# Three engines put in the order of emission, and the w_in conversions cut into five steps: attention, a gated matmul and a soft mixture on one core

## The chip, the cores and the metric

The kernel runs on one core of a Trainium2 chip. The metric is the device time of one execution in microseconds (us); the kernel before was run three times. All times below are of that chip. The engines are TensorE (PE, whose weight loads are listed apart as PEld), VectorE (DVE), ScalarE (ACT), GpSimd (POOL) and SyncE (SP), which here only issues transfers.

## The reference, cut to what matters

```python
# q, k, v: (4, 12, 448, 64) float32; causal attention, then
scores = where(causal_mask, -1e9, q @ k.T / 8)
attn   = exp(scores - max(scores)) / (sum(exp(...)) + 1e-9)
x      = (attn @ v), heads put side by side          # (1792, 768)
h      = x @ w_in                                     # w_in (768, 2048), float64 in memory
g      = maximum(0.01 * h, h)
x      = g @ w_out                                    # w_out (2048, 768), float64 in memory
# soft mixture of 8 experts with 4 slots each
logits = x @ phi                                      # (1792, 32)
d      = softmax over tokens;  slot_input = d.T @ x
slot_out[e] = maximum(slot_input[e] @ w1[e], 0) @ w2[e]
out    = softmax over slots (logits) @ slot_out       # (1792, 768)
```

## The kernel before, in words

**Work.** There are 4 batches of 12 heads. Two heads make a pair, so there are 24 pairs, six to a batch. For a pair `n` the kernel transposes q and k (`qk_stacks`, tile `qkps` in PSUM, `qkt` in SBUF), computes scores once for their maxima (`maxima`: TensorE writes `S`, VectorE reads it into `junk` and the maxima `mxe`), turns the maxima into a row to subtract (`lowering`: `mps`, four ScalarE copies to `mr`), computes transposed scores and their exponentials (`weights`: TensorE writes `T`, ScalarE writes `P`, GpSimd masks the diagonal with an affine select and adds up `tsum`), multiplies by v (`attend`, PSUM tile `O`), inverts the sums (`inverses`: `dn`, a ScalarE copy to `rs`, two VectorE reciprocals) and scales the result into two float16 halves (`columns`: one VectorE product, a ScalarE cast and a GpSimd subtraction into `x`).

**Stages.** Stage 0 does the attention of batch 0. Stages 1, 2 and 3 do the attention of the next batch and, between its parts, `up` of the batch before: 16 column blocks `H` of 18 matmuls each, evacuated by a ScalarE Prelu into `g`. In stages 1 and 2 `g` goes to memory (`g_far`); in stage 3 `up` also adds logits `L` and transposes `g` on VectorE into `g_nat`. After stage 3 come the last `up`, the softmax over tokens, and the experts, whose weights are loaded in 32 transfers of 1.5 MB.

**Slots.** A stage of stages 1 to 3 has 18 slots, three to a pair. I call them A, B and C here. A: `attend(n-1)`, `inverses(n-1)`, `lowering(n)`. B: `maxima` of row block 1, the first part of `weights`, `maxima` of row block 3. C: `columns(n-1)`, the other two parts of `weights`, `maxima` of blocks 0 and 2, `qk_stacks(n+2)`. After each slot follows one column block of `up`, except in the slots 6 and 15 (`GAPS`), which are both slots A.

**Conversions.** w_in and w_out come as float64, and are turned into float32 by integer operations, in 16 units of 128 columns (w_in, names `i0` to `i15`) and 16 of 128 rows (w_out, `o0` to `o15`). `to_f32` does ScalarE Abs (L200) and Sign (L201), for w_in the VectorE maximum (L203), and the VectorE shift (L204) and combination (L205). `prep_in` goes on with `pow2_scale` (a TensorE transposition `w_ps` and five small VectorE operations, L116 to L124), a ScalarE scaling of the sign (L221), a GpSimd product (L222), a ScalarE cast to float16 (L228) and a GpSimd subtraction (L229). `prep_out` multiplies on GpSimd (L238), writes the result to memory, and multiplies it with phi on TensorE (`wt_ps`, `wp_ps`, `wf_ps`) with ScalarE copies between. The units `i6` to `i15` are started in stage 1 (slots 0 to 4 and 6 to 10), `o0` to `o9` in stage 2, `o10` to `o15`, in halves, in stage 3.

**Order.** TensorE runs in the order in which the program emits its instructions: `mm` and `tr` tie each one behind the last. On ScalarE, VectorE and GpSimd a planner sets the order ahead of time, from its own estimate of when each instruction's inputs are ready and from priorities; attention and `up` have a lead of 300 (`AHEAD`). Only the Abs of a conversion (from stage 1 on) and the maximum of v are tied behind what was emitted before them on their engine (`issue_after`). A generator per unit is advanced once per slot by `prep_step`, after the column block; new units are started after that.

**PSUM.** `S` and `T` share two buffers: in a pair they take turns as S(1), T(0), S(3) in slot B and T(1), T(2), S(0,2) in slot C. So S(3) may be written once VectorE has read S(1), and S(0,2) once ScalarE has read T(1). `H` and `O` have one buffer each, and the small tiles (`qkps`, `mps`, `dn`, `w_ps`, `wt_ps` and so on) share two (`TR`).

Of the kernel before, what the change touches and what calls it, by code (L numbers as in the profile page):

```python
# [10 lines left out]
F32 = mybir.dt.float32  # L11
# [23 lines left out]
def tile_attn_moe_softmoe(ctx: ExitStack, tc: tile.TileContext, q, k, v, w_in, w_out, phi, w1, w2, out, dbg=None):  # L35
# [68 lines left out]

    mm = partial(in_order, nc.tensor.matmul)
# [3 lines left out]
    def pow2_scale(absmax, name, shift=23, bias=0, out=None):  # L109
# [6 lines left out]
        nc.vector.tensor_reduce(m1, ps, AX.X, ALU.max)  # L116
        nc.vector.tensor_scalar(m1, m1, as_float((27 + bias) << shift), None, ALU.max)
        e = const.tile([128, 1], I32, tag="p2_e", bufs=2, name=f"{name}_e")
        nc.vector.tensor_scalar(e, m1.bitcast(I32), shift, None, ALU.logical_shift_right)
        si = const.tile([128, 2], I32, tag="p2_s" + name[0], bufs=4, name=f"{name}_s")  # L120
        nc.vector.tensor_scalar(si[:, 0:1], e, -(2**23), (268 + bias) * 2**23, ALU.mult, ALU.add)
        if out is None:
            out = si[:, 1:2].bitcast(F32)
        nc.vector.tensor_scalar(out.bitcast(I32), e, 2**23, -(14 + bias) * 2**23, ALU.mult, ALU.add)  # L124
# [29 lines left out]
    BUFS = ((3, 4, 2), (3, 3, 2), (2, 2, 2))  # L154
# [33 lines left out]
    def to_f32(u, absmax=None):  # L188
# [10 lines left out]
        with tc.issue_after(last_on(mybir.EngineType.Activation)) if stage else ExitStack():  # L199
            nc.scalar.activation(t, hw.bitcast(F32), AF.Abs, scale=2.0**-112)  # L200
        nc.scalar.activation(sg, hw.bitcast(F32), AF.Sign)  # L201
        if absmax is not None:
            nc.vector.tensor_reduce(absmax, t, AX.X, ALU.max)  # L203
        nc.vector.tensor_scalar(ti, ti, 3, None, ALU.logical_shift_left)  # L204
        nc.vector.scalar_tensor_tensor(ti, lw, 29, ti, ALU.logical_shift_right, ALU.bitwise_or)  # L205
# [6 lines left out]
    def prep_in(u):  # L212
# [4 lines left out]
        yield  # L217
        if f >= EARLY[0]:
            yield
        s_w, _ = pow2_scale(am, f"w{f}", 20, out=inv_w[:, f : f + 1])  # L220
        nc.scalar.activation(sg, sg, AF.Copy, scale=s_w)  # L221
        nc.gpsimd.tensor_tensor(t, t, sg, ALU.mult)  # L222
        w = t.rearrange("p (c f) -> p c f", c=NP)
        hi, lo = (w16[f // 4][:, x, :, 128 * (f % 4) : 128 * (f % 4 + 1)] for x in range(2))
        if f < EARLY[0] and f % 4 < HIP:
            nc.gpsimd.tensor_copy(hi, w)
        else:
            nc.scalar.copy(hi, w)  # L228
        nc.gpsimd.tensor_tensor(lo, w, hi, ALU.subtract)  # L229
        ready.add(u[:2])  # L230

    def prep_out(us):

        f, stage = us[0][1], us[0][3]
        wt = None
        for u in us:
            wo, sg = to_f32(u)
            nc.gpsimd.tensor_tensor(wo, wo, sg, ALU.mult)  # L238
# [4 lines left out]
            yield  # L243
            if u[2] is None:
                yield
            if wt is None:
                wt = pools[stage].tile([128, NP, 128], F32, tag="wt", bufs=1, name=f"wt{f}")
            for h in (0, 1) if u[2] is None else (u[2],):
# [18 lines left out]
        ready.add(us[0][:2])  # L267

    ready = set()

    started = [0]
    running = []

# [809 lines left out]
```

## Time and profile before

| | us |
|---|---|
| median of 3 runs | 708.45 |
| the three runs | 708.45, 708.84, 703.36 |
| the profiled execution, its own time | 705.66 |
| its span, first to last instruction | 703.9 |
| TensorE busy (84% of the span) | 592.6 |
| VectorE busy (51%) | 358.0 |
| ScalarE busy (41%) | 289.7 |
| GpSimd busy (34%) | 236.6 |

The mean granted clock of TensorE was 0.951 of full speed. The busy time of an engine is an average over stages that have different limits; a stage is read by who waits for whom in it. In rows of the trace, `xN` is a count, the time in square brackets is the idle time of the engine just ahead of the instruction, and `<-` names what ended it.

### The profile page before, as it was taken

How to read it: one execution, taken by the hardware profiler on the slowest of the kernel's cores; microseconds unless marked ns; L12 is line 12 of the kernel's file. 1: busy time of each engine (PE TensorE's matmuls, PEld its weight loads, DVE VectorE, ACT ScalarE, POOL GpSimd, SP SyncE). 2: the span in 40 equal slices, each digit the busy share in tenths (PEclk: the TensorE clock that was granted, in tenths of full speed). 3: DMA queues.
4: the chain of work that ended last, by engine and by line, in shares of the span. 5: the costliest groups of instructions: out<-in, count | busy, mean ns of one | idle time of the engine just before them, and what ended most of it. 6: DMA issues, size and time to landing. Idle time of an engine off the chain costs nothing.

```text
span 703.9 us, 12298 instructions
## 1 busy us (share of the span) xinstructions
PE 592.6 (84%) x4836; PEld 334.8 (48%) x4836; DVE 358.0 (51%) x884; ACT 289.7 (41%) x571; POOL 236.6 (34%) x247
## 2 busy tenths in 40 slices
PE   3788868877989999899988979999997996998644
PEld 2555544544555555465555545554343443453114
DVE  5868646775764564654645655644555423001004
ACT  1577543656565356465444455442022112011013
POOL 4277743675586342553522434440000000000000
PEclk9999998997989999999999999999999997899798
DMA  9932352542643246663313422206979335999967
GB/s 182 270 99 49 70 173 54 169 129 85 167 145 109 66 150 170 178 189 112 97 49 111 109 81 64 79 24 230 303 279 406 107 146 219 426 423 425 423 259 313
DMA packets 102449, 125.67 MB, mean 179 GB/s; under 512 B 69240, under 2 KB 91256, under 8 KB 98296
## 3 DMA queue, kind: packets, MB, share of 16 engines
q1 hardware_dynamic: 102392, 124.89, 54.2%
q8 instruction: 38, 0.62, 0.4%
q14 instruction: 19, 0.16, 0.1%
HBM read 105.74 MB, written 19.14 MB: 177 GB/s over the span
## 4 chain that ended last, share of the span: by engine, by line
PE 48%; DMA 13%; DVE 11%; ACT 10%; POOL 8%; issue 7%; SPq 1%; ACTq 0%; DVEq 0%; POOLq 0%
PE H L102 22%; DMA w<-in_moe_w_dram 8%; PE O L102 5%; PE g_acc L102 3%; DVE g_nat L608 2%; DVE rs L450 2%; PE S L102 2%; ACT P L408 2%; PE qkps L102 2%; POOL cv_i_None L222 2%; PE ph L941 2%; DMA raw_i_None<-in_moe_w_in_dram 2%; PE dn L102 2%; PE L L102 2%; PE T L102 2%
## 5 line engine op out<-in xcount | busy, mean ns | idle before, releaser
L102 PE MATMUL H<-x,w 128*128 128x448 f16 x1152 | 234.8, 359 | 0.7 <-ACT g L668 0.7
L102 PEld LDWEIGHTS <-w 128*128 128x128 f16 x1152 | 112.5, 100 | 113.4 <-issue 22.5
L372 DVE CUSTOM_DVE_ANT_0 junk<-S,mask 112x224 bf16<-112x224 f32 (+3 forms) x192 | 85.1, 443 | 47.8 <-PE S L102 44.7
L668 ACT ACTIVATE g<-H,iv 128x448 f32<-128x448 f32 x58 | 36.7, 633 | 112.1 <-PE H L102 101.3
L450 DVE RECIPROCAL rs<-rs 128x224 f32<-128x224 f32 x36 | 53.4, 1524 | 38.2 <-ACT rs L448 38.2
L102 PE MATMUL S<-qkt 64*112 64x224 f32 (+3 forms) x192 | 33.8, 393 | 35.0 <-ACT P L408 21.8
L102 PE MATMUL O<-P,v 112*64 112x448 f32 (+3 forms) x384 | 57.4, 444 | 6.1 <-POOL P L412 4.4
L102 PE MATMUL T<-qkt 64*112 64x336 f32 (+3 forms) x576 | 58.4, 315 | 3.9 <-ACT P L408 3.2
L412 POOL TENSOR_SCALAR_AFFINE_SELECT P<-P 112x448 f32<-112x448 f32 x48 | 33.8, 708 | 82.1 <-ACT P L408 69.3
L408 ACT ACTIVATE P<-T 112x672 f32<-112x672 f32 (+1 forms) x72 | 55.8, 791 | 12.1 <-PE T L102 11.8
L485 POOL TENSOR_TENSOR x<-rs,x 128x448 f16<-128x448 f32 x24 | 25.3, 1053 | 84.9 <-ACT x L484 79.6
L102 PEld LDWEIGHTS T<-qkt 64*112 64x112 f32 x576 | 43.1, 180 | 10.4 <-ACT P L408 3.6
L421 POOL TENSOR_TENSOR tsum<-tsum,P 112x448 f32<-112x448 f32 (+1 forms) x48 | 46.4, 967 | 3.1
L102 PEld LDWEIGHTS O<-P,v 112*64 112x64 f32 x384 | 27.5, 148 | 35.2 <-issue 17.6
L1029 PE MATMUL po<-w,hz 128*32 128x384 f32 x256 | 27.3, 548 | 17.7 <-DMA w<-in_moe_w_dram 17.7
L417 POOL TENSOR_TENSOR tsum<-P 112x672 f32<-112x672 f32 x24 | 39.4, 1643 | 1.3
L102 PEld LDWEIGHTS S<-qkt 64*112 64x112 f32 x192 | 16.0, 184 | 50.1 <-ACT P L408 25.6
L933 POOL MEMSET hz<- 128x256 f32 x2 | 0.6, 312 | 109.6 <-PE g_acc L102 109.6
L608 DVE STREAM_TRANSPOSE g_nat<-g 128x448 f32<-128x448 f32 x26 | 16.5, 640 | 37.7 <-ACT g L668 37.7
L350 DVE TENSOR_TENSOR qkt<-qkps,qkt 128x448 fp32r<-128x448 f32 x48 | 28.9, 620 | 10.5 <-ACT qkt L349 10.5
L222 POOL TENSOR_TENSOR cv_i_None<-cv_i_None,cs_i_None 128x768 f32<-128x768 f32 x16 | 28.0, 1747 | 16.8 <-ACT cs_i_None L221 16.8
L384 ACT ACTIVATE mr<-mps,own 128x112 fp32r<-128x112 f32 x96 | 26.2, 361 | 16.0 <-PE mps L102 16.0
(174 smaller groups left out, 865.8 us busy)
## 6 DMA issues: line engine op xcount, KB each, us to landing
w<-in_moe_w_dram SPq DMA_DIRECT2D x32, 1536.0 KB, 20.8
raw_i_None<-in_moe_w_in_dram SPq DMA_DIRECT2D x16, 768.0 KB, 4.6
raw_o_None<-in_moe_w_out_dram SPq DMA_DIRECT2D x10, 768.0 KB, 6.0
g_far<-g SPq DMA_DIRECT2D x32, 224.0 KB, 6.4
gb<-g_far SPq DMA_DIRECT2D x8, 896.0 KB, 6.7
wo<-wsc SPq DMA_DIRECT2D x4, 1536.0 KB, 10.0
qk<-in_q_dram SPq DMA_DIRECT2D x48, 112.0 KB, 2.5
qk<-in_k_dram SPq DMA_DIRECT2D x48, 112.0 KB, 2.9
```

The source lines that it names most:

```text
L102: op(*args, **kwargs)
L222: nc.gpsimd.tensor_tensor(t, t, sg, ALU.mult)
L350: nc.vector.tensor_tensor(st[:, j, 1], p, st[:, j, 0].bitcast(F32), ALU.subtract)
L372: nc.vector.tensor_tensor_reduce(out=junk[:, :w], in0=ps[:, a, at : at + w], in1=mask[:, S - w :], scale=-1.0, scalar=3e38, op0=ALU.add, o ...
L408: nc.scalar.activation(x[:, :, o : o + at], ps[:, :, :at], AF.Exp, scale=SCALE)
L412: nc.gpsimd.affine_select(out=d, in_=d, compare_op=ALU.is_ge, fill=0.0, base=0, pattern=[[0, 4], [1, CP]], channel_multiplier=-1,)
L417: nc.gpsimd.tensor_tensor(tsum[:CP], p[0][:CP, :, 0, CP:], p[0][:CP, :, 1, : S - CP], ALU.add)
L421: nc.gpsimd.tensor_tensor(y, y, p[1][:CP, :, j, : S - CP * (j + 2)], ALU.add)
L450: nc.vector.reciprocal(rs[:, c : c + S // 2], rs[:, c : c + S // 2])
L608: nc.vector.transpose(g_nat[:, :, 32 * f : 32 * (f + n)].rearrange("p c (f x) -> p f c x", x=32), gts[b, f].rearrange("p (c x) -> p c x", ...
L668: nc.scalar.activation(g, ps, AF.Prelu, scale=iv[b][:, f : f + 1], alpha=SLOPE)
L1029: nc.tensor.matmul(po[h][32 * g : 32 * g + 32], hp[:, (t0 + t) % 8], wt[:, t, DH * h - c0 : DH * (h + 1) - c0], start=t0 + t < 4, stop=t0 ...
```

## The change

ScalarE, VectorE and GpSimd instructions go through a wrapper that, from the beginning of stage 1 until the end of stage 3, ties each behind the last one emitted on its engine. In these stages all three engines, like TensorE, run in the order of emission. In stage 0 and after stage 3 the wrapper ties nothing.

`prep_step` gets a phase. In a slot the order of emission is now: the attention part, the steps marked BEFORE, the start of new units, the column block of `up`, the steps marked AFTER. A w_in unit of stage 1 started in slot s does `to_f32` in s, `pow2_scale` in s+1 AFTER, the scaling and the product (L221, L222) in s+3 BEFORE, the cast and the subtraction (L228, L229) in s+4 BEFORE; before, all that follows `to_f32` was done in s+2. A w_in unit of stage 0 does `pow2_scale` in s+1 and the rest in s+2; before, all in s+1. A whole w_out unit does its transpositions one slot earlier, and a w_out unit in halves converts its second half in the next slot BEFORE. The buffers of a conversion in stages 1 and 2 go from 3 to 5 (`cv_t`) and from 2 to 4 (`cv_s`). `columns(n-1)` moves from the beginning of slot C to its end, behind `qk_stacks` and the loads. The slots in which units start are the same as before.

```diff
+    fixed = [False]
+
+    class Ordered:
+        def __init__(self, engine, kind):
+            self.engine, self.kind = engine, kind
+
+        def __getattr__(self, name):
+            op = getattr(self.engine, name)
+
+            def run(*args, **kwargs):
+                with tc.issue_after(last_on(self.kind)) if fixed[0] else ExitStack():
+                    op(*args, **kwargs)
+
+            return run
+
+    scalar = Ordered(nc.scalar, mybir.EngineType.Activation)
+    vector = Ordered(nc.vector, mybir.EngineType.DVE)
+    gpsimd = Ordered(nc.gpsimd, mybir.EngineType.Pool)
...
-    BUFS = ((3, 4, 2), (3, 3, 2), (2, 2, 2))
+    BUFS = ((3, 4, 2), (3, 5, 4), (2, 2, 2))
...
-        with tc.issue_after(last_on(mybir.EngineType.Activation)) if stage else ExitStack():
-            nc.scalar.activation(t, hw.bitcast(F32), AF.Abs, scale=2.0**-112)
-        nc.scalar.activation(sg, hw.bitcast(F32), AF.Sign)
+        scalar.activation(t, hw.bitcast(F32), AF.Abs, scale=2.0**-112)
+        scalar.activation(sg, hw.bitcast(F32), AF.Sign)
...
         t, sg = to_f32(u, am)
-        yield
-        if f >= EARLY[0]:
-            yield
+        yield AFTER
+        yield AFTER
         s_w, _ = pow2_scale(am, f"w{f}", 20, out=inv_w[:, f : f + 1])
-        nc.scalar.activation(sg, sg, AF.Copy, scale=s_w)
-        nc.gpsimd.tensor_tensor(t, t, sg, ALU.mult)
+        yield BEFORE
+        if u[3]:
+            yield BEFORE
+        scalar.activation(sg, sg, AF.Copy, scale=s_w)
+        gpsimd.tensor_tensor(t, t, sg, ALU.mult)
+        if u[3]:
+            yield BEFORE
...
+            wos.append((wo, c0))
+            if u is not us[-1]:
+                yield BEFORE
+        if len(us) == 1:
+            yield AFTER
+        yield AFTER
+        wt = pools[stage].tile([128, NP, 128], F32, tag="wt", bufs=1, name=f"wt{f}")
+        for h in (0, 1):
...
+            if h == 0 and len(us) > 1:
+                yield AFTER
+        yield AFTER
...
-    def prep_step():
-
-        for g in list(running):
-            if next(g, 1) == 1:
-                running.remove(g)
+    def prep_step(phase):
+
+        for x in list(running):
+            if x[1] == phase:
+                x[1] = next(x[0], None)
+                if x[1] is None:
+                    running.remove(x)
...
             yield
-            columns(n - 1)
             if here:
                 weights(n, 1)
                 weights(n, 2)
...
             if n + NP < NPAIR:
                 load_v(n + NP)
+            columns(n - 1)
             if n + NP - 1 < NPAIR:
                 reduce_v(n + NP - 1)
...
             with tc.high_priority(offset=AHEAD):
                 next(slots_of_attention, None)
-                if columns_of_g is not None and x not in GAPS:
+            prep_step(BEFORE)
+            while started[0] < min(count, had + -(-(count - had) * (x + 1) // last)):
+                prep_start()
+            if columns_of_g is not None and x not in GAPS:
+                with tc.high_priority(offset=AHEAD):
                     next(columns_of_g)
-            prep_step()
-            while started[0] < min(count, had + -(-(count - had) * (x + 1) // (slots - (4 if columns_of_g is None or count > NF else 6)))):
-                prep_start()
+            prep_step(AFTER)
...
         load_raw()
+        fixed[0] = True
         for b in range(1, 4):
...
+        fixed[0] = False
```

## Rows read from the trace of the kernel before

**Rows 1.** Busy time by stretch: the transition to stage 1, then stages 1, 2 and 3.

```profile
core 0: us, PE busy (x) PEld busy (x) DVE busy (x) ACT busy (x) POOL busy (x), PEclk, DMA share, GB/s
95.00:109.40 14.40, 9.55 (x89) 7.17 (x89) 6.32 (x21) 6.87 (x13) 5.25 (x7) 0.78 0.63 189
109.40:244.00 134.60, 115.17 (x748) 66.18 (x748) 87.81 (x222) 74.63 (x132) 75.86 (x59) 0.91 0.42 118
244.00:371.10 127.10, 117.77 (x931) 71.08 (x930) 68.16 (x157) 67.41 (x141) 51.97 (x47) 1.00 0.48 135
371.10:481.00 109.90, 101.91 (x782) 58.85 (x782) 61.84 (x134) 52.72 (x117) 39.14 (x43) 1.00 0.28 80
```

**Rows 2.** TensorE's waits in stage 1 and (last) stage 3: total us, times, longest.

```profile
PE S L102 <- ACT P L408: 13.0, 7, 3.0
PE S L102 <- DVE mxe L372: 3.3, 3, 1.5
...
PE S L102 <- ACT P L408: 4.0, 3, 1.5
```

**Rows 3.** Timeline of ScalarE in a slot C of stage 1, and TensorE's wait there.

```profile
145.62 0.88 ACT L200 ACTIVATE cv_i_None<-raw_i_None 128x768 f32<-128x768 f32 x1
...
147.18 0.93 ACT L221 ACTIVATE cs_i_None<-cs_i_None,w_s 128x768 bf16<-128x768 bf16 x1
...
148.19 1.33 ACT L408 ACTIVATE P<-T 112x672 f32<-112x672 f32 x2
...
148.96 0.50 PE L102 MATMUL S<-qkt 64*112 64x112 f32 x4 [3.00 <-ACT P L408]
```

**Rows 4.** Timeline of ScalarE and TensorE at the transition from stage 0.

```profile
102.17 0.89 ACT L201 ACTIVATE cs_i_None<-raw_i_None 128x768 bf16<-128x768 f32 x1 [3.01 <-DMA raw_i_None<-in_moe_w_in_dram]
...
105.14 0.71 ACT L408 ACTIVATE P<-T 112x672 f32<-112x672 f32 x1
...
105.90 0.35 PE L102 MATMUL S<-qkt 64*112 64x224 f32 x2 [2.55 <-ACT P L408]
...
109.44 3.97 PE L102 MATMUL O<-P,v 112*64 112x448 f32 x16 [1.69 <-DVE qkt L350]
```

**Rows 5.** Timeline of TensorE: slot starts and a column block of one pair.

```profile
207.11 2.11 PE L102 MATMUL O<-P,v 112*64 112x448 f32 x16
...
210.06 3.57 PE L102 MATMUL H<-x,w 128*128 128x448 f16 x18
...
213.78 0.36 PE L102 MATMUL S<-qkt 64*112 64x224 f32 x2
...
226.06 2.11 PE L102 MATMUL O<-P,v 112*64 112x448 f32 x16
```

**Rows 6.** What VectorE does for a unit and a pair: timeline and groups, stage 1.

```profile
210.02 0.53 ACT L448 COPY rs<-dn 128x448 f32<-128x448 f32 x1
...
134.44 2.96 DVE L450 RECIPROCAL rs<-rs 128x224 f32<-128x224 f32 x2 [2.51 <-ACT rs L448]
...
131.02 0.29 DVE L116 TENSOR_REDUCE w_m<-w_ps 128x1 f32<-128x128 f32 x1 [0.56 <-PE w_ps L102]
...
131.79 0.14 DVE L124 TENSOR_SCALAR inv_w<-w_e 128x1 int32<-128x1 int32 x1
...
L203 DVE TENSOR_REDUCE w_am<-cv_i_None 128x1 f32<-128x768 f32 x10 | 9.3, 940 | 10.9 <-ACT cv_i_None L200 10.9
...
L204 DVE TENSOR_SCALAR cv_i_None<-cv_i_None 128x768 int32<-128x768 int32 x10 | 8.6, 864 | 0.5
...
L372 DVE CUSTOM_DVE_ANT_0 junk<-S,mask 112x224 bf16<-112x224 f32 x12 | 4.6, 380 | 4.8 <-PE S L102 4.7
```

**Rows 7.** Timeline of GpSimd and VectorE: the same product twice, and a neighbour.

```profile
143.20 1.64 POOL L222 TENSOR_TENSOR cv_i_None<-cv_i_None,cs_i_None 128x768 f32<-128x768 f32 x1 [2.53 <-ACT cs_i_None L221]
...
148.18 2.47 POOL L222 TENSOR_TENSOR cv_i_None<-cv_i_None,cs_i_None 128x768 f32<-128x768 f32 x1 [0.75 <-ACT cs_i_None L221]
148.19 0.96 DVE L205 SCALAR_TENSOR_TENSOR cv_i_None<-raw_i_None,cv_i_None 128x768 int32<-128x768 int32 x1
```

More of the change, by code (lines that the diff above doesn't have):

```diff
@@ L242, in prep_out @@
             )
[L243 to L248, printed above, removed]
-                ps = ps_tr(f"wt_ps{f}_{h}", (128, 3, 128))
-                for j in range(3):
-                    c = 128 * (3 * h + j) - c0
-                    tr(ps[:, j], wo[:, c : c + 128], ident)
-                nc.scalar.copy(wt[:, 3 * h : 3 * h + 3], ps)
-        yield
+            wos.append((wo, c0))
[6 more added lines that the diff above has]
+        for h in (0, 1):
+            wo, c0 = wos[h % len(wos)]
+            ps = ps_tr(f"wt_ps{f}_{h}", (128, 3, 128))
+            for j in range(3):
+                c = 128 * (3 * h + j) - c0
+                tr(ps[:, j], wo[:, c : c + 128], ident)
+            scalar.copy(wt[:, 3 * h : 3 * h + 3], ps)
+            if h == 0 and len(us) > 1:
+                yield AFTER
+        yield AFTER
         psw = ps_tr(f"wp_ps{f}", (96, 128))
@@ L261, in prep_out @@
         w4 = pools[stage].tile([96, 128], F32, tag="w4", bufs=1, name=f"w4_{f}")
-        nc.scalar.copy(w4, psw)
-        yield
+        scalar.copy(w4, psw)
+        yield AFTER
         psf = ps_tr(f"wf_ps{f}", (128, NS))
         mm(psf, w4, istack[:96, :NS], start=True, stop=True)
-        nc.scalar.copy(wprime[:, f], psf)
+        scalar.copy(wprime[:, f], psf)
         ready.add(us[0][:2])
     ready = set()
+    BEFORE, AFTER = "before", "after"
     started = [0]
     running = []
-    def prep_step():
-        for g in list(running):
-            if next(g, 1) == 1:
-                running.remove(g)
+    def prep_step(phase):
[4 more added lines that the diff above has]
+                    running.remove(x)
     def prep_start():
@@ L284, in prep_start @@
         g = prep_in(us[0]) if u[0] == "i" else prep_out(us)
-        next(g)
-        running.append(g)
+        running.append([g, next(g)])
     def need(u):
@@ L330, in reduce_v @@
             v_am[b] = am = const.tile([128, NP + 1], F32, tag="v_am", bufs=2, name=f"v_am{b}")
-            nc.vector.memset(am, 0.0)
-        with tc.issue_after(last_on(mybir.EngineType.DVE)) if b else ExitStack():
-            nc.vector.tensor_reduce(v_am[b][:CP, hp : hp + 1], v_t[n], AX.XY, ALU.max, apply_absolute_value=True)
+            vector.memset(am, 0.0)
+        with tc.issue_after(last_on(mybir.EngineType.DVE)) if b and not fixed[0] else ExitStack():
+            vector.tensor_reduce(v_am[b][:CP, hp : hp + 1], v_t[n], AX.XY, ALU.max, apply_absolute_value=True)
     def v_scale(b):
         am = v_am[b]
-        nc.vector.tensor_reduce(am[:, NP:], am[:, :NP], AX.X, ALU.max)
+        vector.tensor_reduce(am[:, NP:], am[:, :NP], AX.X, ALU.max)
         s_v[b], inv_v[b] = pow2_scale(am[:, NP:], f"v{b}")
@@ L383, in lowering @@
         for i in range(NI):
-            nc.scalar.activation(mr[:, i], ps, AF.Copy, scale=own[:, i : i + 1])
+            scalar.activation(mr[:, i], ps, AF.Copy, scale=own[:, i : i + 1])
     def weights(n, g):
@@ L474, in columns @@
             rs = att.tile([128, S], F32, tag="rs", bufs=1, name=f"rs{n}")
-            nc.scalar.copy(rs, rb)
+            scalar.copy(rs, rb)
         else:
@@ L667, in up @@
             queue.append(f)
[L668 removed]
+            scalar.activation(g, ps, AF.Prelu, scale=iv[b][:, f : f + 1], alpha=SLOPE)
             if far:
@@ L781, in stage @@
         had = started[0]
+        last = slots - (6 if columns_of_g is not None and count <= NF else 4)
         for x in range(slots):
```

127 lines of the change are left out of this document (64 added, 63 removed).

## The prediction, made blind

> **What bounds the kernel now.** I read the busy time by stretch first, then TensorE's waits in each stage, then the timelines of the engines around the longest of them. In stages 1 to 3 TensorE has the most work: 115.2 of 134.6 us, 117.8 of 127.1 and 101.9 of 109.9, while no other of the four is busy for more than 87.8, 68.2 and 61.8 us there [rows 1]. So what the stages can still give is TensorE's idle time, 19.4, 9.3 and 8.0 us, and in stage 1 its clock, 0.91 of full in the mean; it was 1.00 in the other two [rows 1]. After stage 3, from 481 us on, the change ties nothing, so I let that tail move as a whole with the end of stage 3.
>
> The cause of the idle time is visible. TensorE runs in the order written, so a late ScalarE or VectorE result stops all that follows. In stage 1 the wait of S(0,2) for the exponential P is the largest, 13.0 us in 7 waits, and the wait of S(3) for the maxima `mxe` comes next with 3.3 us [rows 2]. A slot C of stage 1 shows the first: ScalarE runs the Abs of a unit and the scaling of another ahead of the two exponentials, which begin at 148.19, and TensorE stands for 3.00 us [rows 3]. The planner had put conversions there. The same happens at the transition: a Sign of a stage 1 unit, which nothing ties, stood in ScalarE's queue in front of an exponential and waited for its transfer [rows 4].
>
> **The transition: about 4.2 us gained.** The Sign waited 3.01 us; the exponential behind it began at 105.14, TensorE waited 2.55 us for it and 1.69 us more ahead of O [rows 4]. With the new order the Sign can't start before the last instruction that stage 0 emitted, so both waits go: 4.2 us. If the exponential finds the next wait at once, only the first goes, 2.5 us. O took 3.97 us there against 2.11 at full clock [rows 4, 5]; if that comes back too the gain is 6.1 us. The granted clock was 0.78 over the whole stretch [rows 1], so I don't count it.
>
> **Stage 1: what goes.** The exponentials now stand ahead of every conversion step of their slot, and the long ScalarE queue in front of them is gone. I take 0.4 us per pair as what is left of that wait, since the exponential follows its scores directly.
>
> **Stage 1: what takes its place.** In the order of emission the VectorE part of a unit started in slot A (L203, L204, L205) and the `pow2_scale` of the unit before stand in front of the maxima of row block 1 in slot B, and S(3) can't be written until these have read S(1). I count from the start of O. A pair with little in its way shows that slot A takes TensorE 6.7 us (207.11 to 213.78) and the pair 18.95 (to 226.06) [rows 5]; less two waits for P of 0.4 us 18.1. The sum copy `rs` starts 2.9 us after O [rows 5, 6]. A copy takes 0.5 and the two reciprocals 2.96, so VectorE has them done at 6.4. L203, L204 and L205 take 0.94, 0.86 and 0.96 [rows 6, 7]: done at 9.2. The five small operations of `pow2_scale` take 0.9 (131.02 to 131.93 [rows 6]): 10.1. Two maxima at 0.38, with their read-outs some 0.45 each [rows 6]: 11.0. TensorE gets to S(3) at 6.7 + 1.2 = 7.9, as S(1) and T(0) take it 1.2. So it waits about 3 us, and H behind it waits as well.
>
> By this I went through the six pairs, with the units that are in each. Pair one (start in slot 0, no `pow2_scale` yet) waits 2.0; pair two 3.0; pair three 5.4, since slot 6 has no column to cover for VectorE, and ScalarE has a cast and a scaling ahead of the Abs; pair four 3.7; pair five, without starts, 0.2; pair six, where slot 15 has no column, 2.7, for the reciprocals alone. Together 17.0. TensorE's own work is six times 18.1 less the two columns that are left out, 3.57 each by the row [rows 5] and 3.4 from start to start: 101.8. To this come 2.4 for the exponentials and 0.9 where `mps` wants the buffer of a `w_ps` that VectorE has not yet read. That makes 122.1 at full clock.
>
> The clock comes on top. [...] Four of the waits above are longer than those of the transition, so 7 to 8 us; I take 7. Stage 1: 129.1 instead of 134.6, **a gain of 5.5 us**. Ends: the waits for the maxima are half as long and the clock stays, 101.8 + 8.5 + 2.4 = 112.7, a gain of 21.9; or every long wait is 1.5 us longer and the clock costs 9, 136, a loss of 1.4.
>
> ScalarE and GpSimd have room: cast, scaling, Abs and Sign cost ScalarE about 0.8 each in sequence (145.62 to 147.18 for two [rows 3]), 3.1 us in a slot of some 6, and a product and a subtraction cost GpSimd 3.3. The five buffers cover the longer life of a unit: started in slot 0 it is ready in slot 4 and wanted in slot 7. That they cost nothing holds as long as the slots keep these lengths; each slot of lateness would use up one of the three in reserve.
>
> **The columns moved to the end of slot C.** Their VectorE product now stands behind the maxima and the two subtractions of `qk_stacks`; the next `attend` needs the buffer O that it reads. Some 2 us of VectorE work follow the transpositions, and the column of 3.4 us covers them. But the cast of `columns` on ScalarE waits for that product, and Abs, Sign and the Prelu of H stand behind it: I find the Prelu late by 1.3 us in slots C with a start.
>
> **Stages 2 and 3: nothing.** In stage 2 w_out units have no L203 and no `pow2_scale`, so S(3) waits 0.2 to 1.2 us in most pairs, and in slots 6 and 15, which have the reciprocals in front as before, 1.0 and 2.5. The late Prelu makes the second `wt_ps` wait for its small buffer, 1.2 to 1.45 us in three slots C. The walk gives 127.5 us against 127.1, so I take 0, with 3 us to either side: below nothing too, as the idle time of 9.3 us [rows 1] could shrink. Stage 3: the waits for P, 4.0 us [rows 2], go, and transpositions of `g` on VectorE, now in fixed places before the maxima, take about as much: 0, again 3 to either side. Stage 0 has its steps moved by a slot and its order made by the planner: 0, 3 to either side.
>
> **SyncE.** The planner still orders the transfers, and every step moved takes its own along. A transfer of `g` waits for a Prelu and holds q and k behind it; those have a whole pair, some 19 us, to arrive. I take 0.
>
> **Sum.** 705.66 - 4.2 - 5.5 = 696.0, made against the profiled execution, which lies 2.8 us below the median of the three runs and between the lowest and the other two. I forecast 696.
>
> **Rivals.**
> *A, the waits go and nothing takes their place (0.20).* If VectorE keeps ahead, stage 1 costs 112.7: 705.66 - 21.9 - 4.2 = 679.6. For it: VectorE is busy for 87.8 of 134.6 us [rows 1], so there is room in the sum. Against it: the room isn't in slot A, where reciprocals, unit and maxima stand in one row.
> *B, an even trade (0.17).* S(3) waits as long as S(0,2) did, the clock falls as often, and only part of the transition is left: 703 to 706.
> *C, slower (0.11).* The maxima of slot B stand behind a unit in stages 2 and 3 too. If a unit ends 1.5 us later there than in my walk, eleven pairs lose 16.5 us: 712.5. From 0.9 us in each pair on (9.7 / 11) the change loses. For it: no start in a slot A can step behind the maxima any more, as the planner let it. Against it: w_out units need only L204 and L205.
> *D, the two engines block each other (0.07).* The same GpSimd product took 1.64 us alone and 2.47 when VectorE began L205 within 0.01 us of it [rows 7]. The new order puts products and subtractions into each slot of a unit's life. If each of the four units started in a slot A finds a whole product of 1.64 us in front of its L205, TensorE loses 6.6 us: 702.6. [...]
>
> **How the numbers follow.** My forecast has 0.45, between 691 and 701. About 1%, 7 us, is what a measurement of this kernel can tell from no change, as its three runs alone differ by 5.5 us. Faster by more: 0.43 of the forecast and all of A, 0.63. Slower by more: 0.09, the larger part of C. Within 1%: 0.28. The range goes from 682, which is nearly A, to 708, which takes in B and D and leaves out most of C.
>
> **What would show it.** In the trace after: at the transition no Sign in front of the exponential, and no wait of 2.5 us there. In stage 1 TensorE's waits for P at 3 us or less in all; its waits for `mxe` at 10 to 20 us, in slots B whose slot A started a unit, longest after slot 6. Stage 1 some 129 us long, its clock still below full; stages 2 and 3 within 3 us of before. The forecast fails if waits for `mxe` stay near 3 us (A), if they appear in stages 2 and 3 at 1.5 us or more per pair (C), or if stage 0 or the tail changes its length by more than 3 us.

## The result and the profile after

The changed kernel takes 689.1 us in the median of four runs (686.7 to 690.9), against 708.6 us of the kernel before: 0.974 of its time, with a 95% interval of 0.968 to 0.979. The forecast was 696.0, with a range of 682 to 708. The profiled execution of the changed kernel took 690.89 us, with a span of 689.2; it is the slowest of its four, and that of before, 705.66, lies below its median. So the two traces differ by 14.7 us, and the medians by 19.5. The account below is that of the traces.

Busy time by stretch, after the change: the transition, then stages 1, 2 and 3 (the columns are those of [rows 1]).

```profile
95.00:105.80 10.80, 8.71 (x91) 6.69 (x91) 5.83 (x20) 5.33 (x11) 5.83 (x7) 0.84 0.77 235
105.80:226.60 120.80, 108.59 (x748) 63.02 (x748) 86.67 (x221) 76.95 (x137) 66.68 (x57) 0.96 0.47 133
226.60:354.80 128.20, 117.32 (x931) 71.06 (x930) 69.50 (x159) 70.00 (x143) 49.70 (x48) 1.00 0.45 134
354.80:466.60 111.80, 105.27 (x782) 59.72 (x782) 61.34 (x134) 52.95 (x118) 39.68 (x44) 0.97 0.27 79
```

Against [rows 1] nearly the whole gain lies in stage 1, which takes 120.8 us instead of 134.6. TensorE's instructions are the same 748, but they take 108.6 us instead of 115.2, as the granted clock is 0.96 instead of 0.91, and its idle time falls from 19.4 to 12.2 us. So of 13.8 us gained some 7 are waiting and some 7 are clock. Stage 1 begins 3.6 us earlier. Stages 2 and 3 are slightly longer, by 1.1 and 1.9 us.

TensorE's waits in stage 1, after the change (total us, times, longest):

```profile
PE S L102 <- ACT P L116: 7.5, 5, 3.5
PE v_ps L102 <- DVE v_am L116: 2.1, 1, 2.1
PE O L102 <- POOL P L116: 1.2, 1, 1.2
PE T L102 <- ACT mr L116: 1.1, 2, 0.5
PE mps L102 <- ACT rs L116: 0.7, 1, 0.7
PE mps L102 <- DVE w_m L116: 0.3, 1, 0.3
```

In the kernel after, L116 is the line of the wrapper, so one goes by the tiles. The wait for P has fallen from 13.0 to 7.5 us [rows 2]. On the timelines, 10.3 of the 13.0 us were waits of S(0,2), in five slots C, and 2.7 were waits of S(3), in two slots B. After the change S(0,2) waits in no slot C, and all five waits for P are those of S(3). The wait for `mxe`, which the forecast put at 17 us, is not there at all. A wait that the forecast didn't know has come: `v_ps` for `v_am`, 2.1 us. The transition and the first slots of stage 1, on the timeline of all engines:

```profile
101.11 0.73 ACT L116 ACTIVATE P<-T 112x672 f32<-112x672 f32 x1 [1.62 <-PE T L102]
...
105.79 2.11 PE L102 MATMUL O<-P,v 112*64 112x448 f32 x16 [1.18 <-POOL P L116]
...
113.45 0.92 ACT L116 ACTIVATE P<-T 112x896 f32<-112x896 f32 x1 [0.40 <-PE T L102]
...
114.42 0.45 PE L102 MATMUL S<-qkt 64*112 64x448 f32 x2 [1.01 <-ACT P L116]
...
114.60 0.38 DVE L116 CUSTOM_DVE_ANT_0 junk<-S,mask 112x224 bf16<-112x224 f32 x1
...
116.78 0.15 DVE L116 TENSOR_REDUCE v_am<-v_am 128x1 f32<-128x6 f32 x1
...
116.99 0.80 PE L102 MATMUL v_ps<-ident,v_am 128*128 128x128 f32 x2 [2.12 <-DVE v_am L116]
```

The exponential of the transition now waits for its scores on TensorE and not behind a Sign, and O begins at 105.79 instead of 109.44, in 2.11 us instead of 3.97 [rows 4]. The lines at 113.45 to 114.60 are one slot B. S(3) is written at 114.42, as the exponential of T(0) ends, and VectorE begins to read S(1) only at 114.60. So S(3) stands in the buffer of T(0), and not in that of S(1). In pairs two, three, four and six it is the same: S(3) is written before VectorE has read S(1). In pair five it is not:

```profile
198.17 0.92 ACT L116 ACTIVATE P<-T 112x896 f32<-112x896 f32 x1 [0.41 <-PE T L102]
...
198.26 0.45 PE L102 MATMUL S<-qkt 64*112 64x448 f32 x2
```

There S(3) is written while ScalarE still reads T(0), so it has the buffer of S(1), which VectorE had read early in this pair without new units.

The longest wait for P that is left is that of the third pair, on ScalarE and TensorE:

```profile
153.63 0.86 ACT L116 CAST w<-cv_i_None 128x768 f16<-128x768 f32 x1
...
154.36 0.97 ACT L116 ACTIVATE cs_i_None<-cs_i_None,w_s 128x768 bf16<-128x768 bf16 x1
...
155.19 0.91 ACT L116 ACTIVATE cv_i_None<-raw_i_None 128x768 f32<-128x768 f32 x1
155.97 0.91 ACT L116 ACTIVATE cs_i_None<-raw_i_None 128x768 bf16<-128x768 f32 x1
...
156.75 0.94 ACT L116 ACTIVATE P<-T 112x896 f32<-112x896 f32 x1
...
157.75 0.71 PE L102 MATMUL S<-qkt 64*112 64x448 f32 x2 [3.46 <-ACT P L116]
```

Four conversion steps stand ahead of the exponential here, 3.1 us in all, after slot 6, which has no column of `up` to cover them.

### The profile page after: what moved, and what is told of

The parts are those of the page before. It is cut to its first block, busy times and chain, and to the rows that moved or that the text cites. A ratio compares the mean times of both kernels' runs of the same rounds, so it can differ in the third digit from the quotient of the medians.

```text
span 689.2 us, 12302 instructions
## 1 busy us (share of the span) xinstructions
PE 590.5 (86%) x4836; PEld 333.7 (48%) x4836; DVE 357.8 (52%) x884; ACT 292.3 (42%) x571; POOL 225.5 (33%) x247
## 4 chain that ended last, share of the span: by engine, by line
PE 57%; DVE 12%; DMA 11%; ACT 7%; POOL 7%; issue 4%; SPq 1%; ACTq 0%; DVEq 0%; POOLq 0%
PE H L102 27%; DMA w<-in_moe_w_dram 8%; PE O L102 5%; PE T L102 3%; PE S L102 3%; PE g_acc L102 3%; DVE rs L116 3%; DVE junk L116 3%; ACT P L116 3%; POOL tsum L116 2%; DVE g_nat L116 2%; PE dn L102 2%; DMA raw_i_None<-in_moe_w_in_dram 2%; PE ph L976 2%; PE L L102 2%
## 5 line engine op out<-in xcount | busy, mean ns | idle before, releaser
L116 DVE CUSTOM_DVE_ANT_0 junk<-S,mask 112x224 bf16<-112x224 f32 (+3 forms) x192 | 85.6, 446 | 78.6 <-PE S L102 73.6
L116 ACT ACTIVATE g<-H,iv 128x448 f32<-128x448 f32 x58 | 36.7, 633 | 107.8 <-PE H L102 83.7
L116 DVE RECIPROCAL rs<-rs 128x224 f32<-128x224 f32 x36 | 53.3, 1523 | 46.5 <-ACT rs L116 46.5
L116 ACT ACTIVATE P<-T 112x672 f32<-112x672 f32 (+1 forms) x72 | 57.1, 793 | 25.8 <-PE T L102 24.8
L116 POOL TENSOR_SCALAR_AFFINE_SELECT P<-P 112x448 f32<-112x448 f32 x48 | 28.4, 592 | 118.4 <-ACT P L116 66.5
L102 PE MATMUL O<-P,v 112*64 112x448 f32 (+3 forms) x384 | 53.1, 417 | 5.6 <-POOL P L116 5.6
L116 POOL TENSOR_TENSOR tsum<-tsum,P 112x448 f32<-112x448 f32 (+1 forms) x48 | 43.2, 899 | 3.3
L1064 PE MATMUL po<-w,hz 128*32 128x384 f32 x256 | 29.2, 580 | 16.4 <-DMA w<-in_moe_w_dram 16.4
L102 PEld LDWEIGHTS O<-P,v 112*64 112x64 f32 x384 | 25.9, 140 | 32.2 <-issue 14.8
L116 POOL TENSOR_TENSOR tsum<-P 112x672 f32<-112x672 f32 x24 | 38.8, 1615 | 1.9
L102 PE MATMUL T<-mr,onesr 64*112 64x448 f32 (+1 forms) x192 | 30.9, 318 | 3.8 <-ACT mr L116 3.8
L116 DVE TENSOR_TENSOR qkt<-qkps,qkt 128x448 fp32r<-128x448 f32 x48 | 27.8, 618 | 10.5 <-ACT qkt L116 10.5
L116 ACT ACTIVATE mr<-mps,own 128x112 fp32r<-128x112 f32 x96 | 26.2, 361 | 14.3 <-PE mps L102 14.3
L116 POOL TENSOR_TENSOR cv_o_None<-cv_o_None,cs_o_None 128x768 f32<-128x768 f32 x10 | 16.5, 1648 | 48.2 <-DVE cv_o_None L116 28.8
L102 PEld LDWEIGHTS S<-qkt 64*112 64x112 f32 x192 | 16.0, 184 | 32.9 <-ACT P L116 13.7
L116 POOL TENSOR_TENSOR w<-cv_i_None,w 128x768 f16<-128x768 f32 x16 | 26.7, 1668 | 10.1 <-ACT w L116 10.0
```

The lines of the kernel that those rows point to most:

```text
L102: op(*args, **kwargs)
L116: op(*args, **kwargs)
L1064: nc.tensor.matmul(po[h][32 * g : 32 * g + 32], hp[:, (t0 + t) % 8], wt[:, t, DH * h - c0 : DH * (h + 1) - c0], start=t0 + t < 4, stop=t0 ...
```

## The experiments

The readings to be told apart were these. The first, of the forecast: what counts is that the exponentials no longer stand behind conversion steps. The first rival: the five steps and the buffers do it, whatever the order. The second: only the transition counts, where one Sign was in the way. A further question is why the waits for `mxe` didn't come. No kernel below leaves out any of the computation.

All eleven experiments beside the two kernels; the lengths are from the traces. The beginning of a stage is that of its first O, in us from the span's start, and stage 3 is counted to the last O. The ratio is to the kernel before, which ran again beside each group of kernels (medians of 707.6 to 708.6 us).

| kernel | median us | ratio (95%) | stage 1 begins | stage 1 | stage 2 | stage 3 |
|---|---|---|---|---|---|---|
| before | 708.6 | | 109.4 | 134.6 | 127.0 | 102.8 |
| after | 689.1 | 0.974 (0.968 to 0.979) | 105.8 | 120.9 | 128.1 | 104.8 |
| order_alone | 792.1 | 1.119 (1.114 to 1.125) | 105.5 | 186.3 | 149.9 | 118.1 |
| steps_alone | 732.1 | 1.037 (1.031 to 1.043) | 110.6 | 131.8 | 137.6 | 118.6 |
| sign_tied | 700.6 | 0.991 (0.988 to 0.994) | 104.3 | 130.6 | 129.8 | 101.8 |
| steps_sign | 707.8 | 1.001 (0.998 to 1.004) | 104.4 | 138.4 | 128.8 | 106.0 |
| stage1_only | 719.0 | 1.015 (1.011 to 1.020) | 103.9 | 121.1 | 144.2 | 117.5 |
| scalar_only | 682.8 | 0.966 (0.960 to 0.972) | 105.6 | 120.8 | 126.2 | 101.4 |
| columns_first | 699.0 | 0.989 (0.982 to 0.995) | 103.7 | 132.0 | 127.1 | 105.1 |
| rotate | 712.6 | 1.005 (1.002 to 1.009) | 113.7 | 132.5 | 132.2 | 103.1 |
| v_early | 678.9 | 0.959 (0.955 to 0.963) | 104.0 | 117.2 | 126.5 | 99.9 |
| scalar_v | 685.2 | 0.967 (0.960 to 0.973) | 105.5 | 118.3 | 126.2 | 101.5 |
| slot5 | 682.4 | 0.963 (0.958 to 0.968) | 104.1 | 120.6 | 126.5 | 99.9 |

**order_alone: the new order with the old steps.** The kernel after, with the steps, the buffers and the place of `columns` of before; the three engines stay in the order of emission.

```diff
-    BUFS = ((3, 4, 2), (3, 5, 4), (2, 2, 2))
+    BUFS = ((3, 4, 2), (3, 3, 2), (2, 2, 2))
...
-        yield AFTER
-        yield AFTER
+        yield
+        if f >= EARLY[0]:
+            yield
         s_w, _ = pow2_scale(am, f"w{f}", 20, out=inv_w[:, f : f + 1])
-        yield BEFORE
-        if u[3]:
-            yield BEFORE
         scalar.activation(sg, sg, AF.Copy, scale=s_w)
         gpsimd.tensor_tensor(t, t, sg, ALU.mult)
-        if u[3]:
-            yield BEFORE
```

> The kernel before with the order of emission alone: its steps, its buffers and the place of the columns as before. Theory 1 (the order alone brings the gain, since it takes the conversions out from in front of the exponentials): 689 to 697. Theory 2 (the order needs the five steps): a unit's scaling, product, cast and subtraction all stand in one slot, and in the order of emission ScalarE's cast waits for GpSimd's product (1.64 us) and the scaling for VectorE, with the next slot's exponentials behind them; 2 to 4 us for each of the ten w_in units: 715 to 735, with the waits of S for P in stage 1 at 20 us or more.

It takes 792.1 us, some 84 more than before and far beyond any of the figures expected. ScalarE in a slot of stage 1, and TensorE's wait there:

```profile
150.08 0.94 ACT L116 ACTIVATE cs_i_None<-cs_i_None,w_s 128x768 bf16<-128x768 bf16 x1 [3.15 <-DVE w_s L116]
...
152.76 0.83 ACT L116 CAST w<-cv_i_None 128x768 f16<-128x768 f32 x1 [1.75 <-POOL cv_i_None L116]
...
155.06 0.90 ACT L116 ACTIVATE P<-T 112x896 f32<-112x896 f32 x1
...
156.02 0.71 PE L102 MATMUL S<-qkt 64*112 64x448 f32 x2 [9.29 <-ACT P L116]
```

Emitted right behind what they need, the scaling waits at the head of ScalarE's queue for VectorE's `w_s`, and the cast for GpSimd's product. The exponential stands behind both, and TensorE waits 9.29 us. In the whole stage its waits for P are 55.6 us in 11 cases, against 7.5 in 5 after. In an order that nothing can step around, each step must find its input ready; that is what the five steps are for. Steps, buffers and the place of `columns` went back together here. columns_first, below, moves only `columns` back and costs 10 us, so most of the loss is that of steps and buffers, which were not taken apart.

**steps_alone: the new steps with the planner's order.** The kernel after without the wrapper's ties; the Abs keeps the tie that it had before.

```diff
-        scalar.activation(t, hw.bitcast(F32), AF.Abs, scale=2.0**-112)
+        with tc.issue_after(last_on(mybir.EngineType.Activation)) if stage else ExitStack():
+            scalar.activation(t, hw.bitcast(F32), AF.Abs, scale=2.0**-112)
...
-        fixed[0] = True
```

> The changed kernel without the order: five steps, more buffers, the columns at the end of slot C, and the planner's order on the three engines, with only Abs and the maximum of v tied as before. Theory 1 (the order brings the gain): 703 to 710. Theory 2 (each half needs the other): 698 to 710, too. Theory 3 (the steps and buffers alone bring it, since no step waits for another engine any more): 687 to 694.

It takes 732.1 us, slower than before, which none of the readings gave; the rival by which the steps alone do it has fallen. Stage 1 is only 2.8 us shorter than before, and stages 2 and 3 are longer by 10.6 and 15.7. ScalarE in stage 2 shows a likely cause, which steps_sign tests:

```profile
263.37 0.89 ACT L116 ACTIVATE cs_o_None<-raw_o_None 128x768 bf16<-128x768 f32 x1 [4.30 <-DMA raw_o_None<-in_moe_w_out_dram]
264.16 0.72 ACT L116 ACTIVATE P<-T 112x672 f32<-112x672 f32 x1
```

This is the Sign of [rows 4] again: untied, it was put in front of an exponential and waited 4.30 us for its transfer.

**sign_tied: the kernel before with one more tie.** The Sign is tied like the Abs, and nothing else is changed.

```diff
-        nc.scalar.activation(sg, hw.bitcast(F32), AF.Sign)
+        with tc.issue_after(last_on(mybir.EngineType.Activation)) if stage else ExitStack():
+            nc.scalar.activation(sg, hw.bitcast(F32), AF.Sign)
```

> The kernel before with the Sign of each conversion of stages 1 to 3 tied behind the last ScalarE instruction emitted, as its Abs is. If the 4 us of the transition come from the Sign alone, O of pair 7 begins 3 to 4.5 us earlier than 109.4 and the time is 702 to 706; if another conversion takes its place in front of the exponential, 707 to 710. Stages 1 to 3 stay within 3 us each.

It takes 700.6 us, less than either figure expected, and the transition is as short as with the whole change:

```profile
99.61 0.73 ACT L409 ACTIVATE P<-T 112x672 f32<-112x672 f32 x1 [1.16 <-PE T L102]
...
104.29 2.11 PE L102 MATMUL O<-P,v 112*64 112x448 f32 x16 [1.18 <-POOL P L413]
```

O begins 5.1 us earlier than before, and stage 1 is 4.0 us shorter. Its waits for P are not: 14.4 us against 13.0. What shrinks is TensorE's busy time, 111.4 us instead of 115.2, at a clock of 0.93 instead of 0.91. Two lines of the source give some 7 of the 19.5 us. The rival "only the transition" accounts for about that part and not for the rest, since stage 1 stays at 130.6.

**steps_sign: the steps, the planner's order, and the Sign tied.** The kernel steps_alone with the tie of sign_tied.

> The changed kernel without the order (as steps_alone), but with the Sign tied as in sign_tied. If steps_alone is slow because the planner puts Signs that wait for their transfers in front of everything on ScalarE: stages 2 and 3 go back to some 128 and 104 us and the time is 700 to 708. If the planner's order on all three engines is at odds with the new steps in other ways too: 715 to 728.

It takes 707.8 us, at the upper end of the lower figure expected. Stages 2 and 3 are back at 128.8 and 106.0, so what steps_alone lost there was the Sign. Stage 1 takes 138.4: with the same steps and buffers the planner's order costs 17.5 us there against the order of emission (120.9). This pair of kernels is the cleanest measure of the order. But it isn't one of exponentials behind conversion steps, as TensorE's waits in stage 1 show (total, times, longest):

```profile
PE S L102 <- ACT P L116: 7.0, 5, 1.7
PE w_ps L102 <- DVE qkt L116: 5.6, 3, 4.7
```

For P TensorE waits no longer than after (7.5). About half of the 17.5 us are other waits, for VectorE and GpSimd, and about half are TensorE's busy time, 117.2 us against 108.6, at a clock of 0.90 against 0.96. The longest wait, on VectorE and TensorE:

```profile
147.81 5.16 DVE L116 SCALAR_TENSOR_TENSOR cv_i_None<-raw_i_None,cv_i_None 128x768 int32<-128x768 int32 x1
...
153.57 0.80 PE L102 MATMUL w_ps<-ident,w_am 128*128 128x128 f32 x2 [4.75 <-DVE qkt L116]
```

A combination that takes 0.96 us in the kernel after takes 5.16 here. GpSimd ran one instruction behind the other meanwhile, four of them until 152.16, and `qkt` stood behind the combination on VectorE.

**stage1_only: the order of emission in stage 1 alone.** The wrapper's ties end with stage 1, and only the Abs stays tied.

```diff
         for b in range(1, 4):
+            if b == 2:
+                fixed[0] = False
```

> The changed kernel with the order ended after stage 1; in stages 2 and 3 the planner sets the order with Abs tied, as before, but with the new steps. If the order costs stages 2 and 3 what they lost (1.1 and 2.0 us): 684 to 688. If the losses come from the new steps or the columns: 688 to 692. If the order is what keeps these stages at their level: 692 to 700.

It takes 719.0 us, outside the figures expected. Stage 1 is that of the kernel after (121.1), and stages 2 and 3 lose 16.1 and 12.7 us. ScalarE waits for the transfers of the Sign, as in steps_alone (total, times, longest):

```profile
ACT cs_o L116 <- DMA raw_o<-in_moe_w_out_dram: 24.9, 10, 4.6
```

In sum these waits are no more than in the kernel before (22.7 us, 12 times), whose stages 2 and 3 are short. What decides is what stands behind them, and that the Sign is the cause is shown by steps_sign alone. So stage1_only does not say what the order is worth in stages 2 and 3. That one reads from steps_sign and after, 128.8 and 106.0 against 128.1 and 104.8: little.

**scalar_only: the order of emission on ScalarE alone.**

```diff
-    vector = Ordered(nc.vector, mybir.EngineType.DVE)
-    gpsimd = Ordered(nc.gpsimd, mybir.EngineType.Pool)
+    vector = nc.vector
+    gpsimd = nc.gpsimd
```

The maximum of v keeps its tie of before.

> The changed kernel with the order on ScalarE alone; VectorE and GpSimd are the planner's again (the maximum of v tied as before). If what counted was what stands in front of the exponentials on ScalarE: 686 to 692. If the order of the other two matters as well, because ScalarE then waits for them at the head of its queue: 695 to 703.

It takes 682.8 us, less than expected, and stage 1 takes 120.8, as with all three engines. The gain there is the order of ScalarE, the engine that writes P. The other two orders add nothing in stage 1, and stages 2 and 3 are 1.9 and 3.4 us shorter without them; what follows stage 3's last O is 3.3 us longer. The four runs (680.2 to 688.7) overlap those of the kernel after, so that the whole is faster is not clear. Against steps_sign, ScalarE's order also took away the long wait for `qkt`; by which of its instructions was not followed.

**columns_first: `columns` back at the beginning of slot C.**

```diff
             yield
+            columns(n - 1)
             if here:
...
-            columns(n - 1)
```

> The changed kernel with the columns back at the beginning of slot C. If the move matters: ScalarE's cast now stands in front of the exponentials and waits for a VectorE product that stands behind the conversions of slot B, 1 to 2 us in each of a dozen pairs, 697 to 708. If it doesn't: 687 to 692, and the waits of wt_ps for the late Prelu in stage 2 (4.9 us) shrink.

It takes 699.0 us, as expected if the move matters; stage 1 takes 132.0. On ScalarE:

```profile
144.08 0.56 ACT L116 CAST x<-rs 128x448 f16<-128x448 f32 x1 [2.27 <-DVE rs L116]
144.55 1.34 ACT L116 ACTIVATE P<-T 112x672 f32<-112x672 f32 x2
```

The cast of `columns` waits 2.27 us for VectorE, and the exponentials of slot C stand behind it. TensorE's waits for P in stage 1 are 15.4 us in 11 cases. Moving `columns` is worth 11 us in stage 1 under this order, not the nothing of the forecast, which only asked what the move costs.

**rotate: S and T in strict turns.** Two tags with one buffer each, used in turns, force the buffers that the forecast assumed.

```diff
+    turn = [0]
...
-        ps = psum.tile([CP, 2, 512], F32, tag="S", bufs=2, name=f"S{n}_{tiles[0]}")
+        turn[0] ^= 1
+        ps = psum.tile([CP, 2, 512], F32, tag=f"S{turn[0]}", bufs=1, name=f"S{n}_{tiles[0]}")
...
-        ps = psum.tile([CP, 2, 512], F32, tag="S", bufs=2, name=f"T{n}_{g}")
+        turn[0] ^= 1
+        ps = psum.tile([CP, 2, 512], F32, tag=f"S{turn[0]}", bufs=1, name=f"T{n}_{g}")
```

> The changed kernel with the two buffers of S and T taking turns by hand (a tag of one buffer each), so that S(3) gets the buffer of S(1) in every pair, as the prediction took for granted. If that was the step that failed: TensorE waits 13 to 20 us for mxe in stage 1 instead of none, and the time is 697 to 706. If VectorE is ahead in any case: no such waits, 687 to 691.

TensorE's waits for `mxe` in stage 1 of this kernel, from its timeline:

```profile
123.36 0.45 PE L102 MATMUL S<-qkt 64*112 64x448 f32 x2 [2.06 <-DVE mxe L116]
...
148.36 0.45 PE L102 MATMUL S<-qkt 64*112 64x448 f32 x2 [2.42 <-DVE mxe L116]
...
171.55 0.71 PE L102 MATMUL S<-qkt 64*112 64x448 f32 x2 [5.73 <-DVE mxe L116]
...
196.38 0.45 PE L102 MATMUL S<-qkt 64*112 64x448 f32 x2 [2.95 <-DVE mxe L116]
...
234.19 0.46 PE L102 MATMUL S<-qkt 64*112 64x448 f32 x2 [2.24 <-DVE mxe L116]
```

The forecast's walk had 2.0, 3.0, 5.4, 3.7, 0.2 and 2.7 for the six pairs, 17.0 in all. Measured are 2.06, 2.42, 5.73, 2.95, none and 2.24, 15.4 in sum. So the walk was right for strict turns, and the kernel after takes them in one pair of six only. The columns behind these five waits take 5.16 to 5.81 us, 8.9 more than at 3.57 each, where 7 was forecast. Stage 1 takes 132.5 us, where the forecast had 129.1. The whole kernel, at 712.6, is slower than expected, since stage 0 is 8 us longer too, and stage 2 is 4: in stage 0 T waits 8.7 us in 5 cases for `mxe`, against 0.6 in one in the kernel after.

**v_early: the late wait that the forecast didn't know.** The last reduction of `v_am` is emitted with the last part of v instead of right before TensorE transposes it, behind a slot's maxima.

```diff
+        if hp == NP - 1:
+            am = v_am[b]
+            vector.tensor_reduce(am[:, NP:], am[:, :NP], AX.X, ALU.max)
...
-        vector.tensor_reduce(am[:, NP:], am[:, :NP], AX.X, ALU.max)
```

> The changed kernel with the last small maximum of v (over six columns) emitted with the last reduction of the batch, a pair earlier. The three waits of v_ps for it (2.1, 1.6 and 1.6 us) go: 5.3 us, 683 to 686. If TensorE then waits for something else in the same slots, 687 to 691.

The same slot as at 114.42 to 117.58 after:

```profile
112.59 0.46 PE L102 MATMUL S<-qkt 64*112 64x448 f32 x2 [1.01 <-ACT P L116]
112.98 0.49 PE L102 MATMUL v_ps<-ident,v_am 128*128 128x128 f32 x2
113.31 3.57 PE L102 MATMUL H<-x,w 128*128 128x448 f16 x18
```

and the column that followed the wait in the kernel after:

```profile
117.58 4.84 PE L102 MATMUL H<-x,w 128*128 128x448 f16 x18
```

The wait of 2.12 us is gone, and the column behind it takes 3.57 us instead of 4.84. With 678.9 us this is the lowest median of all, 1.5% below that of the kernel after, and beats both kernels. The three waits for `v_am` were 5.2 us; 10.2 us are gained, more than expected. In the traces stages 1 to 3 give 3.7, 1.7 and 4.9 us of it; in stage 3 the clock goes from 0.97 to 1.00 with one wait of 1.56 us removed.

**scalar_v and slot5: is there more?** scalar_v joins scalar_only and v_early. slot5 takes v_early and starts the unit of slot 6 one slot earlier, so that no start falls into the slot without a column:

```diff
-            while started[0] < min(count, had + -(-(count - had) * (x + 1) // last)):
+            extra = 1 if count == NF and x == 5 else 0
+            while started[0] < min(count, had + extra + -(-(count - had) * (x + 1) // last)):
```

> The changed kernel with the order on ScalarE alone (as scalar_only) and the small maximum of v emitted early (as v_early). If VectorE's order cost scalar_only's rival only the three waits of v_ps, both edits do the same thing and the time is that of v_early within 4 us, 676 to 683. If GpSimd's and VectorE's order cost something beside: 671 to 675.

> v_early with the unit that starts in slot 6 started in slot 5 instead, so that the slot A without a column has no Abs, Sign and VectorE part of a unit. The wait of S(3) for P of 3.5 us there shrinks to 1 to 2 us and the slow column behind it (4.9 instead of 3.6 us) may come back to full clock: 675 to 677. If the work only moves on and slot 7 pays: 678 to 680.

Neither gains, and both lie above every figure expected of them. scalar_v takes 685.2 (681.5 to 690.7), no less than scalar_only and 6.3 more than v_early (678.1 to 680.0). So what the orders of VectorE and GpSimd seemed to cost in stages 2 and 3 was the late `v_am`, and once that is early, leaving the two to the planner loses 6 us. In the traces over half of this, 4.5 us, lies behind stage 3's last O; why was not followed. slot5 takes 682.4, 3.5 more than v_early. In it the wait of 3.46 us for P shrinks to 1.01, and others come in its place:

```profile
147.88 0.31 PE L102 MATMUL mps<-ident,mxe 112*128 112x112 f32 x1 [1.19 <-ACT rs L116]
...
149.51 0.80 PE L102 MATMUL w_ps<-ident,w_am 128*128 128x128 f32 x2 [1.32 <-DVE w_m L116]
...
153.28 0.71 PE L102 MATMUL S<-qkt 64*112 64x448 f32 x2 [1.01 <-ACT P L116]
...
153.92 6.24 PE L102 MATMUL H<-x,w 128*128 128x448 f16 x18
```

1.19, 1.32 and 1.01 make 3.52: the waits only moved to the slot before. The rest is the clock, 0.94 in stage 1 instead of v_early's 0.97, with 2.7 us more of TensorE's busy time.

## Why the forecast was right, and which step of it failed

**The number: in the range, in part by luck.** The direction and the cause named for it, conversion steps in front of exponentials, were right. But 689.1 lies below the 691 to 701 of my own forecast, and its terms were off both ways: stage 1 gained 13.7 us and not 5.5, and stages 2 and 3 lost 3.0 and not 0. With the first alone put right the sum is 688, with both 691. That the result lies within 682 to 708 says little for the walk, as that range reaches nearly to A. Of the signs named, the transition without a Sign in front came, and stages 2 and 3 within 3 us. The waits for `mxe` in stage 1 (10 to 20 us, measured 0), those for P (3 us or less, measured 7.5) and a stage 1 of 129 us (measured 120.9) did not.

**The transition: right.** 4.2 us were forecast, and O begins 3.65 us earlier. sign_tied shows the cause by itself. How exact that is stays open: after, stage1_only and columns_first emit stage 0 the same way and begin stage 1 between 103.7 and 105.8.

**"The exponentials now stand ahead of every conversion step": right as the cause, too good in size.** The waits of S(0,2) for P, 10.3 us before, are 0 after, and ScalarE's order alone has none either. But the 0.4 us per pair that I left for P, 2.4 in all, are 7.5: four waits of 1.01 for the exponential of T(0), whose buffer S(3) takes, and the 3.46 of the third pair, where the exponential stands behind four conversion steps after all. And it is not all that the order is worth: steps_sign waits no longer for P than the kernel after and is 17.5 us longer in stage 1, for waits on VectorE and GpSimd and for the clock.

**"S(3) can't be written until these have read S(1)": this step failed.** It rested on the S and T tiles taking strict turns. They share two buffers, but which one a tile gets is not bound to the order of the program; in the kernel after S(3) stands in the buffer of T(0) in five pairs of six. That is shown by the times at 114.42 and 114.60. It could have been read before the change. In three pairs of the kernel before S(3) did wait for `mxe` [rows 2], but in the third and the sixth it waited for the exponential of T(0):

```profile
164.52 0.71 PE L102 MATMUL S<-qkt 64*112 64x448 f32 x2 [1.71 <-ACT P L408]
```

VectorE read the second half of S(1) only from 165.18 on. I had put all seven waits for P down to S(0,2), and had let the tiles take turns in all pairs. Of the "two waits for P of 0.4 us" in the pair that the walk was measured by, one was S(3)'s for `mxe` (0.39). The term of 17.0 us had the right size for strict turns, as rotate shows pair by pair, and is 0 here. How the buffers are chosen, and why more pairs took the other one after the change, was not tried.

**The clock: right in kind, 7 us forecast, about 4.3 measured.** Three columns behind waits took 4.84, 4.90 and 5.26 us instead of 3.57, 4.3 us in sum; the granted clock was 0.73, 0.72 and 0.68 in them, and 1.00 in the first column of the stage. No run shows the term of 7 us, an estimate from what O took more at the transition [rows 4, 5]: 4.3 us came here, and 8.9 in rotate. I had expected four long waits; there were two in slots B, of 2.12 and 3.46 us, and the third slow column came after waits of 0.54 and 1.01 in a row. Put together, the walk for stage 1 was 101.8 of work, 20.3 of waits and 7 of clock, 129.1. Measured are 11.7 of waits within the stage (the 12.9 of the view less O's 1.2, which lies ahead of its first O) and 4.3 of clock; with 101.8 that is 117.8, and 3.1 of the 120.9 stay unassigned.

**Stages 2 and 3: "nothing", and 1.1 and 1.9 us measured.** The late Prelu was right: 1.2 to 1.45 us in three slots C were forecast for the second `wt_ps`, and 0.98, 1.43 and 1.43 came. The waits for `mxe` were 1.8 us in stage 2 and 2.2 in stage 3, smaller than the walk. What the forecast missed is one wait of 1.56 us for `v_am` in each of the two. The move of that reduction behind a slot's maxima stood in the diff's order of emission, and I walked through conversions only. v_early shows that the three waits for `v_am`, that of stage 1 included, cost 10 us with the clock behind them.

**The columns.** That the move costs little was right (stage 2 is 1.0 us shorter in columns_first); that it is worth 11 us in the new order was not seen. The walk took slot C's exponentials as first in their slot, which they are only because `columns` has left it.

**The rivals.** A (679.6) comes nearest to what the waits for `mxe` did, but its terms don't hold either: P kept 7.5 us, VectorE was not ahead but S(3) stood elsewhere, and A's 112.7 still holds 8.5 us of waits for the maxima, which its words rule out. B and C didn't happen. D went the other way: the products and the combinations took less time than before (below). The forecast's 696 is 7 us above the median, and 5 above the profiled execution with which its sum was made.

## What to carry to other kernels

An order of emission that nothing can step around pays on the engine that feeds the bounding one (here ScalarE, which writes P), and only if no step reaches the head of its queue before its input is there: with the same ties it was 0.97 of the time with the work cut into steps, and 1.12 with the old steps, buffers and place of `columns`. Before an instruction is costed as waiting for a buffer, read from the trace, in every pair, which tile the buffer was last used by; two tiles under one tag need not take turns. And for every small instruction between two engines, ask what now stands ahead of it: a reduction of 0.15 us behind four maxima, three times in the run, cost 10 us.

## What the runs showed of the hardware that was not expected

GpSimd's products and VectorE's combinations took less time, although the steps were spread over more slots. Groups of instructions of stage 1 (total us, mean ns, idle time before), in the kernel before:

```profile
L222 POOL TENSOR_TENSOR cv_i_None<-cv_i_None,cs_i_None 128x768 f32<-128x768 f32 x10 | 18.1, 1806 | 13.5 <-ACT cs_i_None L221 13.5
...
L205 DVE SCALAR_TENSOR_TENSOR cv_i_None<-raw_i_None,cv_i_None 128x768 int32<-128x768 int32 x10 | 11.4, 1148 | 0.1
```

and in the kernel after:

```profile
L116 POOL TENSOR_TENSOR cv_i_None<-cv_i_None,cs_i_None 128x768 f32<-128x768 f32 x10 | 16.5, 1647 | 8.2 <-ACT cs_i_None L116 8.2
...
L116 DVE SCALAR_TENSOR_TENSOR cv_i_None<-raw_i_None,cv_i_None 128x768 int32<-128x768 int32 x10 | 9.6, 958 | 0.3
```

Ten products take 1647 ns in the mean instead of 1806, and the combinations 958 instead of 1148: 3.5 us less in all, and the means are now those of the shorter times in [rows 7] (1.64 and 0.96 us). Instruction by instruction, each of the ten products takes 1.64 to 1.66 us after and each combination 0.96, and no product runs beside a combination. In the kernel before, the two products of 2.47 us, at 148.18 [rows 7] and 198.35, began within 0.01 us of a combination; the other eight ran beside none and took 1.64. Where the planner orders VectorE and GpSimd, single combinations of stage 1 take up to 2.31 us (scalar_only) and 5.16 (steps_sign). What made these longer was not shown. A longer combination need not cost time: scalar_only's stage 1 is as short as that of the kernel after.

The price of waiting on TensorE was more than the wait itself in several places: a column of 3.57 us took 4.84 us behind a wait of 2.12 and 4.90 behind one of 3.46, at a granted clock of 0.73 and 0.72, and 6.24 in slot5 behind three waits of 1.0 to 1.3. Behind a single wait of 1.01 us two columns took 3.58, at a clock of 1.00, no longer than in a pair without waits [rows 5]. Where between these the clock falls was not settled.
